# Fewer, larger transfers at both ends of a decode kernel, and a table load ahead of small transfers

## The chip, the cores and the metric

One core of a Trainium2 chip. The metric is device microseconds of one execution. The result is compared with executions of the kernel before made on the same chip in the same call (one batch of kernels, timed together). "Span" is the profiled time on the core, some 2 us shorter than the device time.

## The reference

A decode step for a batch of 8 (width 448): attention over the last 1024 positions of a key and value cache, a small MLP on the normalised input, and a gate that mixes the two.

```python
q = x @ wq                                   # 16 heads of 256
k, v = k_cache[:, :, -1024:], v_cache[:, :, -1024:]   # 8 kv heads, bf16
o = softmax(q k^T / 16) v                    # two query heads share one kv head
a = o.reshape(8, 4096) @ wo                  # wo: 4096 x 448
b = gelu(layernorm(x) @ w1 + b1) @ w2 + b2
out = g * a + (1 - g) * b,   g = sigmoid(sum(x * gate_w))
```

Keys and values are 67 MB, the weights wq, w1, w2 and wo 10.6 MB. All of it is read once.

## The kernel before

Every large load goes through a ring of nine slots of 128 x 8192 bf16, issued by the sync engine as slots come free. Keys and values come as 32 slots ("units") of 2 MB. The parts that the change touches:

```python
    WO_PARTS = [[(0, 4), (4, 8)]] * 2 + [            # row blocks of each quarter of wo,
        [(0, 4), (4, 6), (6, 8)],                    # 11 transfers in all
        [(0, 4), (4, 6), (6, 7), (7, 8)],
    ]
    ...
    add(("wq", 0), rows_loader([wq_m[:, 0 : 2 * HD]]))
    add(("wq", 1), rows_loader([wq_m[:, 2 * HD : 3 * HD], wq_t]))
    add_kv("k", A_k_cache, 0, parts=2)               # first keys in two halves
    ...                                              # w1, w2, then keys and values in turn
    for u in range(NQ - LAG, NQ):
        add_kv("v", A_v_cache, u, parts=2 if u == NQ - 1 else 1)   # last values in two halves
    ...
    pump()                                           # sync engine: issue what has a slot
    nc.scalar.dma_start(x_sb[:], xf)                 # ScalarE: four small transfers
    ...                                              # gate weights, b2, b1
    # GpSimd meanwhile: masks, and a long memset of qw
    # norm_and_gate():
        nc.vector.memset(eps_t[:], 1e-5)
        nc.scalar.activation(rstd[:], mv[:, 1:2], ACT.Sqrt, bias=eps_t[:], scale=1.0)
    ...
    # the end of the program
    values(u)                                        # last values
    gather(u)
    project(0, 0, 4)                                 # each piece of wo as it lands
    keep_clock(A_hi[:, W // 2 : W], 1)               # filler matmuls into an unused bank
    project(0, 4, NJ8)
    ...
    project(3)
    nc.vector.tensor_copy(res[:, 0:DH2], halves[0])
    nc.scalar.copy(res[:, DH2:D], halves[1])
    nc.sync.dma_start(out_f, res[:])
```

One thing that the source does not show: the built program gives each transfer, from either engine, one of eight completion semaphores in turn. A transfer waits until the earlier one with its semaphore has landed, so at most eight are under way: in the kernel before, for instance, the transfer issued at 176.51 us has the semaphore on which the last values landed at 176.49.

Of the kernel before, what the change touches and what calls it, by code (L numbers as in the profile page):

```python
# [8 lines left out]
ACT = mybir.ActivationFunctionType  # L9
# [3 lines left out]
F32 = mybir.dt.float32  # L13
# [5 lines left out]
def kernel(  # L19
# [15 lines left out]
    nc = tc.nc  # L35
    P = nc.NUM_PARTITIONS

    NB, Sq, D = A_x.shape
# [4 lines left out]
    W = min(4096, max(256, Sk // 4))  # L43
# [16 lines left out]
    NQ = NB * Hkv // QUAD  # L60
# [6 lines left out]
    HPQ = 4  # L67
    NHQ = Hq // HPQ
    NJ8 = HPQ * NJ
    WO_PARTS = [[(0, 4), (4, 8)]] * 2 + [  # L70
        [(0, 4), (4, 6), (6, 8)],
        [(0, 4), (4, 6), (6, 7), (7, 8)],
    ]
    RING = 9
    LAG = 2
    NK = 4
# [10 lines left out]
    consts = ctx.enter_context(tc.tile_pool(name="consts", bufs=1))  # L87
# [13 lines left out]
    def pump():  # L101
        while len(slots) < min(len(plan), consumed[0] + RING):
            t = ring.tile([P, SLOT], BF16, tag="slot", name="slot")
            plan[len(slots)](t)
            slots.append(t)
# [5 lines left out]
    def kv_loader(src, u, parts):  # L111
        b, half = divmod(u, Hkv // QUAD)
        v = src[b, half * QUAD : (half + 1) * QUAD, kv_base:Sk, :].rearrange(
            "a (s c) d -> s a (c d)", c=NCK
        )

        def load(t):
            n = NCK * Dh // parts
            for i in range(parts):
                nc.sync.dma_start(  # L120
                    t[:, i * n : (i + 1) * n], v[:, :, i * n : (i + 1) * n]
                )

        return load

    def rows_loader(pieces):
        def load(t):
            o = 0
            for ap in pieces:
                n = 1  # L130
                for s in ap.shape[1:]:
                    n *= s
                dst = t[:, o : o + n]
                if len(ap.shape) == 3:
                    dst = dst.rearrange("p (a n) -> p a n", a=ap.shape[1])
                nc.sync.dma_start(dst, ap)
                o += n

        return load
# [3 lines left out]
    def add(key, loader):  # L143
        index[key] = len(plan)
        plan.append(loader)

    def add_kv(name, src, u, parts=1):
        add((name, u), kv_loader(src, u, parts))
# [7 lines left out]

    add(("wq", 0), rows_loader([wq_m[:, 0 : 2 * HD]]))
    add(("wq", 1), rows_loader([wq_m[:, 2 * HD : 3 * HD], wq_t]))
    add_kv("k", A_k_cache, 0, parts=2)
    add(("w1",), rows_loader([w1_m, w1_t]))  # L160
    add(("w2",), rows_loader([w2_v]))
    for u in range(1, NQ):
# [1 line left out]
        if u >= LAG:  # L164
            add_kv("v", A_v_cache, u - LAG)
    for u in range(NQ - LAG, NQ):
        add_kv("v", A_v_cache, u, parts=2 if u == NQ - 1 else 1)
    for q in range(0, NHQ, 2):
        add(
            ("wo", q),  # L170
# [3 lines left out]
                    for i in range(2)  # L174
                    for j0, j1 in WO_PARTS[q + i]
                ]
# [3 lines left out]
    def slot(*key):  # L180
        return slots[index[key]]

    consts.tile([P, 112], BF16, name="pad")
    x_sb = consts.tile([NB, D], BF16)
    pump()
    nc.scalar.dma_start(x_sb[:], xf)
    gw_b = consts.tile([NB, D], BF16)
# [45 lines left out]
    def transposed(dst, src, srcz):  # L233
        tp = ps_misc.tile([P, NX, NB], BF16, tag="misc", name="tp")
        for r in range(NR):
            nc.tensor.transpose(tp[:, r, :], src[:, r:DM:NR], ident[:NB, :NB])
        for h in range(2):
            nc.tensor.transpose(tp[:, NR + h, :], srcz[:, h, :], ident[:NB, :NB])
        nc.vector.tensor_copy(dst[:], tp[:])
# [51 lines left out]
    def norm_and_gate():  # L291
        stats = consts.tile([NB, nc.vector.BN_STATS_DIM], F32)
        nc.vector.bn_stats(stats[:], x_sb[:])  # L293
        mv = consts.tile([NB, nc.vector.BN_AGGR_DIM], F32)
        nc.vector.bn_aggr(mv[:], stats[:])
        eps_t = consts.tile([NB, 1], F32)
        nc.vector.memset(eps_t[:], 1e-5)
        rstd = consts.tile([NB, 1], F32)
        nc.scalar.activation(rstd[:], mv[:, 1:2], ACT.Sqrt, bias=eps_t[:], scale=1.0)
        nc.vector.reciprocal(rstd[:], rstd[:])  # L300
        y_sb = consts.tile([NB, D], BF16)
        nc.vector.tensor_scalar(
            y_sb[:],
            x_sb[:],
            scalar1=mv[:, 0:1],
            scalar2=rstd[:],
            op0=ALU.subtract,
            op1=ALU.mult,
        )
        for h in range(2):  # L310
            nc.vector.tensor_copy(yz[:, h, h::2], y_sb[:, DM:D])
        transposed(yT, y_sb, yz)
        prod = consts.tile([NB, D], F32)
        gl = consts.tile([NB, 1], F32)
        nc.vector.scalar_tensor_tensor(
            prod[:],
            in0=x_sb[:],
            scalar=1.0,
            in1=gw_b[:],
            op0=ALU.mult,  # L320
            op1=ALU.mult,
            accum_out=gl[:],
        )
        gth = consts.tile([NB, 1], F32)
        nc.scalar.activation(gth[:], gl[:], ACT.Tanh, scale=0.5)
        nc.vector.tensor_scalar(
            gg[:, 0:1], gth[:], 0.5, 0.5, op0=ALU.mult, op1=ALU.add
        )
        nc.vector.tensor_scalar(
            gg[:, 1:2], gth[:], -0.5, 0.5, op0=ALU.mult, op1=ALU.add  # L330
        )
        nc.gpsimd.memset(each[:], 1.0)
        nc.vector.tensor_scalar_mul(each[:, 0:NB], ident[0:NB, 0:NB], gg[:, 0:1])
        gp = ps_misc.tile([P, NB], F32, tag="misc", name="gp")
        nc.tensor.matmul(  # L335
            gp[:], lhsT=each[:, NB : NB + P], rhs=each[:, 0:NB], start=True, stop=True
        )
        nc.vector.tensor_copy(gg_s[:], gp[:])
# [163 lines left out]
    def gather(u):  # L502
        first = soft.pop(u)
        os_ = epool.tile([P, Dh], F32, tag="os", name="os_")
        nc.vector.scalar_tensor_tensor(
            os_[:],
            in0=PO[:, 1, :],
            scalar=own[:, 1:2],
            in1=first[:],
            op0=ALU.mult,  # L510
            op1=ALU.add,
        )
        soft[u] = os_

    def finish(u):
        b, half = divmod(u, Hkv // QUAD)
        os_, rs = soft.pop(u), rsel.pop(u)
        sm = ps_sm.tile([P, NJ, RQ], F32, tag="sm", name="fin")
        for j in range(NJ):
            nc.tensor.matmul(  # L520
                sm[:, j, :], lhsT=os_[:, j::NJ], rhs=rs[:], start=True, stop=True
            )
        nc.scalar.activation(  # L523
            oT[:, half * RQ : (half + 1) * RQ, :, b].rearrange("p h j -> p j h"),
            sm[:],
            ACT.Copy,
            scale=gg_s[:, b : b + 1],
        )
# [64 lines left out]
    def keep_clock(dst, n):  # L593
        for _ in range(n):
            nc.tensor.matmul(dst, lhsT=foreign[:], rhs=place[:], start=True, stop=True)

    norm_and_gate()
    query()
    for hf in range(NH):
# [26 lines left out]
    u = NQ - 1  # L626
    A_lo = ps_misc.tile([NB, DH2], F32, tag="misc", name="A_lo")
    A_hi = ps_s.tile([P, W], F32, tag="S", name="A_hi")
# [15 lines left out]
    def spread_rows(q0, q1):  # L644
        pp = ps_sm.tile([P, HPQ, NJ, q1 - q0, NB], F32, tag="sm", name="pp")
        for i in range(HPQ):
            for m in range(HPQ):
                nc.tensor.matmul(
                    pp[32 * i : 32 * i + 32, m],
                    lhsT=ident[:, m::HPQ],  # L650
                    rhs=oTv[:, i, :, q0:q1, :],
                    start=True,
                    stop=True,
                )
        nc.vector.tensor_copy(
            oP[:, :, q0:q1, :], pp[:].rearrange("p m j q b -> p (m j) q b")
        )

    def project(q, j0=0, j1=NJ8):
        w = slot("wo", q - q % 2)  # L660
        for j in range(j0, j1):
            o = ((q % 2) * NJ8 + j) * D
            for i, dst in enumerate(halves):
                nc.tensor.matmul(  # L664
                    dst,
                    lhsT=oP[:, j, q, :],
                    rhs=w[:, o + i * DH2 : o + (i + 1) * DH2],
                    start=False,
                    stop=(q == NHQ - 1 and j == NJ8 - 1),
                    skip_group_check=True,  # L670
                )
# [19 lines left out]
    keep_clock(A_hi[:, W // 2 : W], 4)  # L691
    values(u)
    gather(u)
    project(0, 0, 4)
    keep_clock(A_hi[:, W // 2 : W], 1)
    project(0, 4, NJ8)
    finish(u)
    project(1, 0, 4)
    spread_rows(HALF, NHQ)
    project(1, 4, NJ8)  # L700
    keep_clock(A_hi[:, W // 2 : W], 1)
    project(2)
    keep_clock(A_hi[:, W // 2 : W], 1)
    project(3)

    nc.vector.tensor_copy(res[:, 0:DH2], halves[0])
# [32 lines left out]
```

## Time and profile before

| | |
|---|---|
| time, median of 3 | 190.5 us (190.38 to 190.54) |
| span of the profiled run | 188.4 us |
| bytes of the loads' queue | 77.67 MB |
| rate in the middle of the run | 429 to 432 GB/s |
| first large packet starts | 1.76 us |
| last completion of the output weights | 185.43 us |

The page of the kernel before lists issues by size, with the median time from issue to landing; these are the ones that the change merges:

```profile
q1 hardware_dynamic: 7360, 77.67, 97.3%
...
slot<-in_A_wo_dram SPq DMA_DIRECT2D x6, 448.0 KB, 26.5
...
slot<-in_A_k_cache_dram SPq DMA_DIRECT2D x2, 1024.0 KB
slot<-in_A_v_cache_dram SPq DMA_DIRECT2D x2, 1024.0 KB
```

The first line is the queue of the sync engine: packets, MB, and packet time as a share of 16 engines' span. Its 97.3% leave 5 us of the span, which are the start-up and the end. The 26.5 us from issue to landing is queueing: a piece of 0.45 MB takes about 1.1 us when its turn comes. The prediction shows the other lines.

### The profile page before, as it was taken

Reading aid. Unit: us, or ns where it says so; the run is one execution under the profiler, and the core shown is the slowest. Engines: PE = TensorE matmul, PEld = TensorE weight load, DVE = VectorE, ACT = ScalarE, POOL = GpSimd, SP = SyncE. Lnnn points to the kernel's source line nnn. Section 1 sums busy time; section 2 is a strip of 40 time slices with the busy share of each in tenths; the row PEclk is TensorE's granted clock in tenths of the full one; section 3 lists DMA queues with packets and bytes.
Section 4 is the critical chain, followed back from the end, with each engine's and each line's share of the span. In section 5 each row is a group of like instructions: output and inputs, shape, how many; then the busy total and the mean of one; then the engine's idle time right before and its main releaser. Section 6 shows DMA issues by size and latency. Waiting matters only on the chain.

```text
span 188.4 us, 2359 instructions
## 1 busy us (share of the span) xinstructions
PE 140.2 (74%) x945; PEld 70.3 (37%) x945; DVE 128.6 (68%) x178; ACT 45.1 (24%) x92; POOL 6.6 (4%) x14
## 2 busy tenths in 40 slices
PE   0027978998987589986758596849795999898983
PEld 0011863344434243433233243315242534345451
DVE  6960378979989494949494949595867768695300
ACT  2032220041340404040404040402240041325300
POOL 8500000000000000000000000000000000000000
PEclk9999999999999965799999699988999579999998
DMA  6999999999999999999999999999999999999991
GB/s 217 410 419 434 428 441 430 428 425 438 431 425 428 438 431 428 425 438 428 428 431 437 418 435 431 435 425 431 428 438 425 431 431 438 418 430 418 412 396 49
DMA packets 7548, 77.83 MB, mean 413 GB/s; under 512 B 985, under 2 KB 1778, under 8 KB 2674
## 3 DMA queue, kind: packets, MB, share of 16 engines
q1 hardware_dynamic: 7360, 77.67, 97.3%
q8 instruction: 7, 0.11, 0.2%
q10 hardware_dynamic: 178, 0.02, 0.1%
q14 instruction: 3, 0.02, 0.0%
HBM read 77.68 MB, written 0.01 MB: 412 GB/s over the span
## 4 chain that ended last, share of the span: by engine, by line
DMA 82%; DVE 9%; PE 4%; ACT 2%; issue 1%; DVEq 0%; SPq 0%; ACTq 0%
DMA slot<-in_A_k_cache_dram 59%; DMA slot<-in_A_v_cache_dram 18%; DMA slot<-in_A_wo_dram 4%; DVE kt L346 2%; DVE xz L242 2%; PE Sq L360 2%; ACT qw L401 1%; DMA x_sb<-in_A_x_dram 1%; DVE qw L403 1%; PE A_lo L664 1%; PE qt L375 1%; ACT qs L370 1%; PE qp L388 1%; PE gp L335 0%; DVE stats L293 0%
## 5 line engine op out<-in xcount | busy, mean ns | idle before, releaser
L346 DVE STREAM_TRANSPOSE kt<-slot 128x2048 int32<-128x2048 int32 x32 | 73.7, 2306 | 29.4 <-DMA slot<-in_A_k_cache_dram 29.4
L418 PE MATMUL S<-kt,qw 128*128 128x512 bf16 x256 | 69.4, 418 | 23.7 <-DVE kt L346 23.2
L418 PEld LDWEIGHTS <-qw 128*128 128x128 bf16 x256 | 26.4, 103 | 62.8 <-issue 41.9
L523 ACT ACTIVATE oT<-fin,gg_s 128x16 bf16<-128x16 f32 x16 | 5.2, 328 | 73.2 <-PE fin L520 73.2
L447 ACT ACTIVATE E<-S,nmx 128x1024 bf16<-128x1024 f32 x16 | 22.2, 1389 | 1.8 <-DVE nmx L444 1.7
L430 DVE TENSOR_REDUCE mx<-S 128x1 f32<-128x1024 f32 x16 | 19.0, 1188 | 0.1
L490 PE MATMUL PO<-slot,ET 128*16 128x512 bf16 x256 | 18.3, 410 | 0.3 <-DMA slot<-in_A_v_cache_dram 0.3
L499 ACT ACTIVATE first<-PO,own 128x256 f32<-128x256 f32 x16 | 7.6, 473 | 28.1 <-PE PO L490 28.1
L412 PE MATMUL S<-place,foreign 128*128 128x512 bf16 x32 | 13.4, 418 | 0.1
L460 DVE STREAM_TRANSPOSE ET<-E 128x512 int32<-128x512 int32 x16 | 11.2, 697 | 2.2 <-ACT E L447 2.2
L438 PE MATMUL mz<-m,same 128*128 128x4 f32 x32 | 6.4, 271 | 5.6 <-ACT oT L523 5.4
L438 PEld LDWEIGHTS mz<-m,same 128*128 128x128 f32 x32 | 5.2, 203 | 7.4 <-ACT oT L523 6.6
L471 PEld LDWEIGHTS den<-rowsum,rowden 128*128 128x128 f32 x32 | 6.7, 215 | 3.3 <-issue 1.0
L490 PEld LDWEIGHTS <-ET 128*16 128x16 bf16 x256 | 5.2, 91 | 5.3 <-issue 1.8
L412 PEld LDWEIGHTS <-foreign 128*128 128x128 bf16 x32 | 3.3, 102 | 9.2 <-issue 7.6
L664 PE MATMUL A_lo<-slot,oP 128*8 128x224 bf16 x32 | 4.8, 257 | 1.5 <-DMA slot<-in_A_wo_dram 1.2
L403 DVE CAST qw<-qp 32x512 bf16<-32x512 f32 x4 | 2.7, 687 | 3.4 <-ACT qw L401 3.4
L471 PE MATMUL den<-rowsum,rowden 128*128 128x1 f32 x32 | 5.0, 227 | 0.0
L482 ACT ACTIVATE rsel<-sel,rb 128x8 f32<-128x8 f32 x16 | 4.7, 292 | 1.0 <-DVE rb L481 1.0
L664 PE MATMUL A_hi<-slot,oP 128*8 128x224 bf16 x32 | 4.9, 259 | 0.0
L242 DVE COPY xz<-x_sb 8x64 bf16<-8x64 bf16 x2 | 4.1, 4030 | 0.5 <-DMA x_sb<-in_A_x_dram 0.5
L379 DVE COPY qd<-qt 128x64 bf16<-128x64 bf16 x4 | 0.6, 218 | 5.5 <-PE qt L375 5.5
(143 smaller groups left out, 105.3 us busy)
## 6 DMA issues: line engine op xcount, KB each, us to landing
slot<-in_A_k_cache_dram SPq DMA_DIRECT2D x15, 2048.0 KB, 36.9
slot<-in_A_v_cache_dram SPq DMA_DIRECT2D x15, 2048.0 KB, 36.8
slot<-in_A_wo_dram SPq DMA_DIRECT2D x6, 448.0 KB, 26.5
slot<-in_A_wq_dram SPq DMA_DIRECT2D x1, 2048.0 KB, 7.6
slot<-in_A_k_cache_dram SPq DMA_DIRECT2D x2, 1024.0 KB
slot<-in_A_v_cache_dram SPq DMA_DIRECT2D x2, 1024.0 KB
slot<-in_B_w_dram SPq DMA_DIRECT2D x1, 1568.0 KB
slot<-in_B_w_dram SPq DMA_DIRECT2D x1, 1344.0 KB, 11.8
```

The source lines that it names most:

```text
L242: nc.vector.tensor_copy(xz[:, h, h::2], x_sb[:, DM:D])
L346: nc.vector.transpose(kt[:].rearrange("p c k x r -> p (c k x r)").bitcast(WORD), kn[:, hf * CH * Dh : (hf + 1) * CH * Dh].bitcast(WORD),)
L412: nc.tensor.matmul(S[u][:, cols], lhsT=foreign[:], rhs=place[:], start=True, stop=False)
L418: nc.tensor.matmul(S[u][:, cols], lhsT=qw[:, j, u, m * RQ : m * RQ + P], rhs=kt[:, :, k, :, par], start=False, stop=(k == NK - 1 and par = ...
L430: nc.vector.reduce_max(mx[:], S[u][:], axis=AXIS.X)
L438: nc.tensor.matmul(mz[:], lhsT=same[:], rhs=m4[:], start=True, stop=True)
L447: nc.scalar.activation(E[:].rearrange("p c x i -> p c i x"), S.pop(u)[:].rearrange("p (c i x) -> p c i x", i=PAIR, x=BLK), ACT.Exp, bias=n ...
L460: nc.vector.transpose(ET[:].rearrange("p c r i -> p (c r i)").bitcast(WORD), E[:].rearrange("p c x i -> p (c x i)").bitcast(WORD),)
L471: nc.tensor.matmul(den[u][:], lhsT=rowden[:], rhs=rowsum[:], start=True, stop=True)
L490: nc.tensor.matmul(PO[32 * t : 32 * t + PAIR * RQ], lhsT=ET[:, c, 0:RQ, :], rhs=vn[:, PAIR * c * Dh : PAIR * (c + 1) * Dh], start=(c < QUA ...
L499: nc.scalar.activation(first[:], PO[:, 0, :], ACT.Copy, scale=own[:, 0:1])
L664: nc.tensor.matmul(dst, lhsT=oP[:, j, q, :], rhs=w[:, o + i * DH2 : o + (i + 1) * DH2], start=False, stop=(q == NHQ - 1 and j == NJ8 - 1), ...
```

## The change

The intent: larger transfers where the stream looked least efficient (the output weights), one transfer less at each end of the cache, and the table that Sqrt needs loaded before ScalarE begins its small transfers. With coarser weights, the end of the program is put in a simpler order.

```diff
-    WO_PARTS = [[(0, 4), (4, 8)]] * 2 + [
-        [(0, 4), (4, 6), (6, 8)],
-        [(0, 4), (4, 6), (6, 7), (7, 8)],
-    ]
+    WO_PARTS = [[(0, 8)]] * 3 + [[(0, 6), (6, 8)]]
@@
-    add_kv("k", A_k_cache, 0, parts=2)
+    add_kv("k", A_k_cache, 0)
@@
-        add_kv("v", A_v_cache, u, parts=2 if u == NQ - 1 else 1)
+        add_kv("v", A_v_cache, u)
@@
+    eps_t = consts.tile([NB, 1], F32)
+    rstd = consts.tile([NB, 1], F32)
+    nc.gpsimd.memset(eps_t[:], 1e-5)
+    nc.scalar.activation(rstd[:], eps_t[:], ACT.Sqrt)
     pump()
     nc.scalar.dma_start(x_sb[:], xf)
@@ (eps_t and its memset on VectorE, rstd: removed from norm_and_gate)
@@
-    project(0, 0, 4)
-    keep_clock(A_hi[:, W // 2 : W], 1)
-    project(0, 4, NJ8)
+    keep_clock(A_hi[:, W // 2 : W], 3)
     finish(u)
-    project(1, 0, 4)
+    project(0)
     spread_rows(HALF, NHQ)
-    project(1, 4, NJ8)
-    keep_clock(A_hi[:, W // 2 : W], 1)
+    project(1)
+    keep_clock(A_hi[:, W // 2 : W], 3)
     project(2)
-    keep_clock(A_hi[:, W // 2 : W], 1)
+    keep_clock(A_hi[:, W // 2 : W], 2)
     project(3)
```

More of the change, by code (lines that the diff above doesn't have):

```diff
@@ L295, in norm_and_gate @@
         nc.vector.bn_aggr(mv[:], stats[:])
-        eps_t = consts.tile([NB, 1], F32)
-        nc.vector.memset(eps_t[:], 1e-5)
-        rstd = consts.tile([NB, 1], F32)
         nc.scalar.activation(rstd[:], mv[:, 1:2], ACT.Sqrt, bias=eps_t[:], scale=1.0)
@@ L657, in spread_rows, with project @@
         )
-    def project(q, j0=0, j1=NJ8):
+    def project(q):
         w = slot("wo", q - q % 2)
-        for j in range(j0, j1):
+        for j in range(NJ8):
             o = ((q % 2) * NJ8 + j) * D
```

## The prediction

> **What bounds the kernel now.** I read the page from the top: busy shares first, then the slices, then the chain, and only then the timeline of the head and of the tail, because the change touches nothing in between.
>
> ```profile
> PE 140.2 (74%) x945; PEld 70.3 (37%) x945; DVE 128.6 (68%) x178; ACT 45.1 (24%) x92; POOL 6.6 (4%) x14
> ...
> DMA  6999999999999999999999999999999999999991
> GB/s 217 410 419 434 428 441 430 428 425 438 431 425 428 438 431 428 425 438 428 428 431 437 418 435 431 435 425 431 428 438 425 431 431 438 418 430 418 412 396 49
> ...
> DMA 82%; DVE 9%; PE 4%; ACT 2%; issue 1%; DVEq 0%; SPq 0%; ACTq 0%
> ```
>
> No compute engine is over 74%. The DMA row is 9 in every slice between the first and the last, and the chain that ended last is 82% transfers. So 77.67 MB (the bytes of queue q1 on the page) through the 16 DMA engines set the time, and compute only follows. The windows show how full the stream is, and where it is not at its best:
>
> ```profile
> 60.00:100.00 40.00, 30.59 (x186) 14.54 (x186) 29.17 (x33) 9.29 (x20) 0.00 (x0) 0.87 1.01 432
> ...
> 176.50:183.00 6.50, 5.62 (x83) 3.32 (x83) 0.78 (x2) 0.80 (x2) 0.00 (x0) 1.00 1.03 407
> ```
>
> The last two columns are DMA share and GB/s. In the stretch of keys and values the engines are full (1.01) at 432 GB/s; in the stretch of the output weights they are as full (1.03), yet move 407. Full but slower means a cost per packet, not a wait. After the stream comes only a short tail:
>
> ```profile
> 184.83 0.26 PE L664 MATMUL A_lo<-slot,oP 128*8 128x224 bf16 x1
> ...
> 185.19 0.26 PE L664 MATMUL A_lo<-slot,oP 128*8 128x224 bf16 x1
> ...
> 185.48 0.26 PE L664 MATMUL A_lo<-slot,oP 128*8 128x224 bf16 x1
> ...
> 185.77 0.38 DVE L706 CAST res<-A_lo 8x224 bf16<-8x224 f32 x1 [4.74 <-PE A_hi L664]
> 185.80 0.34 ACT L707 CAST res<-A_hi 8x224 bf16<-8x224 f32 x1 [5.54 <-PE A_hi L664]
> 186.22 0.35 SPq L708 DMA_DIRECT2D out_dram<-res  x1
> ```
>
> Each of those matmuls starts as its own small piece of weights lands (the trace counts the last completion of the last piece at 185.43 us). From there to the end of the span, 188.4 us, are 2.9 us that the change leaves alone but for the last matmuls. The head looks like this:
>
> ```profile
> 0.73 0.58 ACTq L186 DMA_DIRECT2D x_sb<-in_A_x_dram  x1
> 0.73 1.35 SPq L136 DMA_DIRECT2D slot<-in_A_wq_dram  x3
> ...
> 2.36 1.28 ACT L299 ACT_TABLE_LOAD   x1 [2.36 <-issue]
> 2.61 4.35 POOL L289 MEMSET qw<- 128x5120 bf16 x1
> ...
> 2.95 4.10 DVE L242 COPY xz<-x_sb 8x64 bf16<-8x64 bf16 x2 [0.48 <-DMA x_sb<-in_A_x_dram]
> ...
> 10.46 0.29 ACT L299 ACTIVATE rstd<-mv,eps_t 8x1 f32<-8x1 f32 x1 [6.81 <-DVE eps_t L297]
> ```
>
> The table load ends at 3.64 us, and its user runs at 10.46: the load is already hidden. The two tiny copies of x start at 2.95 us and end only at 7.06, 0.1 us after GpSimd's long memset of qw (2.61 + 4.35 = 6.96).
>
> **What the Trainium skill says.** (1) "DMA: Bandwidth & Descriptors", section "Bandwidth", asks for transfers of 1 MiB or more and puts a floor of about 10.5 ns on a packet; section "Why small descriptors are slow (HBM only)" names a fixed cost per packet. The trace agrees in kind and shows a smaller number: packets of 16384, 8192, 3584, 1792 and 896 bytes took 611, 309, 141, 75 and 42 ns (medians of the packet records), which is about 7 to 9 ns plus 36.9 ps per byte. (2) The same page, section "Queues, rings and completion order", says that an engine takes turns between the rows of its queues, a packet at a time. The trace agrees: the 28-byte packets of b1 sit between large ones, and the gate weights, issued at 1.35 us, have most of their packets only at 5.6 to 6.8 us, behind weights of wq that were queued before them. (3) "SBUF — State Buffer", section "Who interferes with whom": a VectorE copy in a two-port mode and a GpSimd operation exclude each other for a whole instruction. The 4.03 us for an 8x64 copy, ending with the memset, agree. (4) "ScalarE: Activation LUTs", section "What ACT_TABLE_LOAD costs", gives 1283 ns; both loads here took 1283 ns.
>
> **The change part by part.**
>
> *Transfers.* Output weights go from 11 to 5, first keys and last values from 2 to 1 each: 8 transfers fewer. Every transfer has a row per partition, 128 packets, so 8 per engine, plus one completion packet per engine of 9 ns. (Check: 51 loads x (128 + 16) and 16 completions of the store are 7360, the page's count for q1.)
> - Output weights, before, per engine: 8 x (6 x 140.7 + 3 x 74.6 + 2 x 41.6) ns = 9.21 us, with the mean times of the packet records.
> - After: rows of 7168 and 5376 bytes, which the line above puts at 271 and 205 ns: 8 x (3 x 271 + 205 + 75) ns = 8.75 us. Gain 0.46 us.
> - Keys and values in one: 2 x 8 x (2 x 309 - 611) ns = 0.11 us. Eight completion packets: 8 x 9 ns = 0.07 us.
> - Sum of packet times: 0.64 us.
>
> Packets overlap a little (shares of 1.01 to 1.03), so this is an upper figure. A lower one comes from landings: the output weights took 176.49 to 185.43 us = 8.94 us, and their 3.67 MB at 430 GB/s would take 8.53. That excess of 0.41 us belongs to 88 data and 11 completion packets less the 16 or so that keys and values have for as many bytes, so about 5 ns each; 72 packets per engine fewer (64 data, 8 completion) give 0.36 us. I take the middle, **0.5 us**, and all of it lies on the stream, which is the path.
>
> *The tail.* The last piece holds two row blocks instead of one: one more pair of matmuls, 0.09 us apart in the timeline, after the last landing. **+0.1 us.** The projection of the third part now waits for a whole 0.9 MB, but 16 matmuls take some 0.8 us and such a part lands every 2.1 us, so TensorE catches up each time. The first six blocks of the last part take 6 x 0.095 = 0.57 us, about what the last piece takes to land (0.60 us), so they just fit. Fillers in this stretch grow from 3 to 8 matmuls of 0.21 us, which fill waits and keep the clock.
>
> *The last values in one.* The first half of that matmul group could start a half transfer earlier before; but the trace shows all 16 starting at 176.55, after both halves. Cost 0.
>
> *The head.* ScalarE now does a table load (1.28 us) and one small activation (0.29 us) before it issues x: at about 0.73 + 1.6 = 2.35 us instead of 0.73. By then wq is queued, so x waits behind it as the gate weights did (over 4 us): I expect it to land at 6.5 to 7.5 us instead of 2.85. Most of this is free, because the copies of x are held until 7.06 us by the memset anyway; the first query matmul loses 0 to 0.8 us. This is hidden: the key transfer that follows the head in the chain is issued at 31.19 and lands at 64.35, so 33 us of transfers are queued ahead of it. The early table load saves nothing on the path. Moving x away from the front of the queues could start wq earlier by up to 0.1 us (its first packets start at 1.76 us, those of x at 1.68); I count 0.
>
> Total: -0.5 + 0.1 = **-0.4 us**, 190.5 to 190.1.
>
> **The rivals.** *A larger gain, by 1 us or more:* if each transfer cost a fixed setup on the stream, 8 fewer would give it. Against it: the engines are full to 1.03 in that very stretch, so completions of one transfer overlap the next one. It would give 189.5. *The late x becomes the bound:* x, then wq's release, then later issues. For it: x is on the chain at its start, and eight semaphores shared by all transfers make later issues wait for earlier landings, now also for the late small ones. Against it: four transfers (5.8 MB) are queued before the first such wait, good for over 13 us. It would give 190.5 to 191.5. *Coarse pieces stall the end:* TensorE idles, its clock halves, and the last six blocks plus two take twice as long: +0.8 us, so 190.8. Against it: the granted clock was 1.00 up to 186 us and the fillers increase.
>
> **Range and chances.** The packet estimate runs from 0.36 to 0.64 us, the tail may cost 0 to 0.4, and the three runs before spread by 0.16 us. Predicted 190.1 us, eight times in ten within 189.6 to 190.5. Two per cent are 3.8 us, more than the whole tail after the stream; nothing in the change reaches that either way: faster 0.01, same 0.98, slower 0.01.
>
> **What would show it.** Right: queue q1 with 1152 packets fewer (6208); the stretch of output weights above 415 GB/s; last landing near 185.0 instead of 185.43 us; x landing after 6 us with the first key transposes at most 1 us later, and the GB/s row unbroken. Wrong: a hole in the DMA row near 10 to 30 us (the late x reached the stream), a granted clock under 1 after 178 us, or a last landing that has not moved, which would say that the packet cost was not on the slowest engine's path.

## The result, and the profile after

190.14 us median (189.78 to 190.49, four runs) against 190.52 (190.38 to 190.61, four runs). The ratio is 0.9981, 95% interval 0.9961 to 1.0000: same at two per cent. Ratios here are the mean time of one kernel's runs over that of the other's runs of the same rounds, so they are not quite the ratio of the medians. Later: 190.29 against 190.44 and 190.21 against 190.42. Over the 14 executions, the differences of the means are 0.37, 0.17 and 0.22 us, on average **0.24 us** weighted by runs.

The page of the changed kernel, against the rows in the prediction: rates, the loads' queue and the chain.

```profile
GB/s 210 417 435 428 436 425 426 432 432 432 428 428 435 428 435 428 428 432 428 432 437 425 421 439 435 421 432 439 425 425 435 439 428 425 425 442 432 409 392 38
...
q1 hardware_dynamic: 6208, 77.67, 97.1%
...
DMA 76%; DVE 15%; PE 4%; ACT 2%; issue 1%; DVEq 0%; ACTq 0%; SPq 0%
```

Same bytes in 6208 packets instead of 7360, and no hole in the stream. The chain's share of transfers falls from 82% to 76% and that of VectorE rises from 9% to 15%. That is no shift of the bound: the chain goes back through whichever event released each slot, and the rates of the stream are unchanged. The windows of the changed kernel, with DMA share and GB/s last:

```profile
60.00:100.00 40.00, 29.39 (x187) 14.25 (x189) 29.09 (x33) 9.63 (x21) 0.00 (x0) 0.89 1.01 430
...
176.50:183.00 6.50, 4.89 (x73) 2.92 (x75) 0.78 (x2) 0.81 (x2) 0.00 (x0) 1.00 1.00 416
```

The middle is as before; the stretch of the output weights rises from 407 to 416 GB/s. The head, in order of time (start, duration, engine; ACTq and SPq are the sequencers that issue transfers):

```profile
0.73 1.28 ACT L185 ACT_TABLE_LOAD   x1 [0.73 <-PEq L719]
...
0.86 0.58 ACTq L187 DMA_DIRECT2D x_sb<-in_A_x_dram  x1
...
2.03 0.20 ACT L185 ACTIVATE rstd<-eps_t 8x1 f32<-8x1 f32 x1
...
2.65 4.36 POOL L290 MEMSET qw<- 128x5120 bf16 x1
...
4.58 2.51 DVE L243 COPY xz<-x_sb 8x64 bf16<-8x64 bf16 x2 [2.10 <-DMA x_sb<-in_A_x_dram]
...
7.38 0.18 DVE L240 COPY xT<-tp 128x40 bf16<-128x40 bf16 x1 [0.28 <-PE tp L239]
```

The issue of x starts at 0.86 us, *while* the table load runs (0.73 to 2.01), not after it. Even so x lands at 4.5 us instead of 2.85: it now stands behind the first packets of wq, which take 1.0 to 1.7 us each at the start (packet records), where before it was 0.08 us ahead of them. The copies of x still end at 7.09 us, when the memset ends at 7.01, so the transposed x is ready at 7.56 instead of 7.51.

The tail, the projection of the last quarter:

```profile
184.69 0.26 PE L662 MATMUL A_lo<-slot,oP 128*8 128x224 bf16 x1
...
185.26 0.26 PE L662 MATMUL A_lo<-slot,oP 128*8 128x224 bf16 x1
...
185.35 0.26 PE L662 MATMUL A_lo<-slot,oP 128*8 128x224 bf16 x1
...
185.65 0.38 DVE L702 CAST res<-A_lo 8x224 bf16<-8x224 f32 x1 [4.96 <-PE A_hi L662]
```

The six-block piece has landed by 184.65 and the last piece at 185.18 (completion records). The first six blocks just fit between; the last two follow at 185.26 and 185.35. The copy of the result starts at 185.65 instead of 185.77 us: 0.12 us gained, which is 0.25 at the last landing less 0.13 for the extra block behind it.

### The profile page after: what moved, and what is told of

The parts are those of the page before. It is cut to its first block, busy times and chain, and to the rows that moved or that the text cites. A ratio compares the mean times of both kernels' runs of the same rounds, so it can differ in the third digit from the quotient of the medians.

```text
span 188.2 us, 2351 instructions
## 1 busy us (share of the span) xinstructions
PE 132.2 (70%) x938; PEld 68.0 (36%) x950; DVE 126.7 (67%) x177; ACT 45.4 (24%) x93; POOL 6.7 (4%) x15
## 3 DMA queue, kind: packets, MB, share of 16 engines
q1 hardware_dynamic: 6208, 77.67, 97.1%
## 4 chain that ended last, share of the span: by engine, by line
DMA 76%; DVE 15%; PE 4%; ACT 2%; issue 1%; DVEq 0%; ACTq 0%; SPq 0%
DMA slot<-in_A_k_cache_dram 40%; DMA slot<-in_A_v_cache_dram 20%; DMA slot<-in_A_wo_dram 15%; DVE kt L344 7%; DMA x_sb<-in_A_x_dram 2%; PE Sq L358 2%; DVE xz L243 1%; ACT qw L399 1%; DVE mx L428 1%; DVE qw L401 1%; ACT qs L368 1%; PE A_lo L662 0%; PE qp L386 0%; PE qt L373 0%; DVE ET L458 0%
## 5 line engine op out<-in xcount | busy, mean ns | idle before, releaser
L416 PE MATMUL S<-kt,qw 128*128 128x512 bf16 x256 | 66.0, 402 | 31.0 <-DVE kt L344 28.5
L416 PEld LDWEIGHTS <-qw 128*128 128x128 bf16 x256 | 25.6, 100 | 66.3 <-issue 43.9
L488 PE MATMUL PO<-slot,ET 128*16 128x512 bf16 x256 | 17.5, 395 | 0.3 <-DMA slot<-in_A_v_cache_dram 0.3
L410 PE MATMUL S<-place,foreign 128*128 128x512 bf16 x25 | 9.8, 390 | 0.1
L410 PEld LDWEIGHTS <-foreign 128*128 128x128 bf16 x32 | 3.2, 99 | 8.6 <-issue 6.9
L662 PE MATMUL A_lo<-slot,oP 128*8 128x224 bf16 x32 | 3.7, 258 | 1.2 <-DMA slot<-in_A_wo_dram 1.1
L290 POOL MEMSET qw<- 128x5120 bf16 x1 | 4.4, 4355 | 0.0
L593 PEld LDWEIGHTS <-foreign 128*128 128x128 bf16 x33 | 2.9, 99 | 3.6 <-issue 0.8
L593 PE MATMUL idle<-place,foreign 128*128 128x512 bf16 x16 | 4.1, 378 | 0.1
```

Source lines behind the costliest of these rows:

```text
L410: nc.tensor.matmul(S[u][:, cols], lhsT=foreign[:], rhs=place[:], start=True, stop=False)
L416: nc.tensor.matmul(S[u][:, cols], lhsT=qw[:, j, u, m * RQ : m * RQ + P], rhs=kt[:, :, k, :, par], start=False, stop=(k == NK - 1 and par = ...
L488: nc.tensor.matmul(PO[32 * t : 32 * t + PAIR * RQ], lhsT=ET[:, c, 0:RQ, :], rhs=vn[:, PAIR * c * Dh : PAIR * (c + 1) * Dh], start=(c < QUA ...
L593: nc.tensor.matmul(dst, lhsT=foreign[:], rhs=place[:], start=True, stop=True)
```

## The experiments

**Theory A:** the stream of transfers is full, each packet costs it about 5 ns, and the change takes away 72 packets per engine (64 data, 8 completion); nothing else in it matters but one more pair of matmuls at the end. **Rivals:** F, a fixed cost per transfer; H, the head carries the gain or loses some; N, scatter; and, for the end, that fillers keep the clock up. V came up on the way: something in the combination makes the weights alone slower.

A single execution scatters by 0.2 us or more, about as much as the effect. So beside the time I read one number from the completion records of each trace: when the 16 DMA engines each finish the last piece of output weights, as mean, and as the slowest of the 16, which is the one that the matmuls wait for.

| run | large transfers | mean engine, us | slowest engine, us | median, us (before) |
|---|---|---|---|---|
| before | 51 | 184.52 | 185.43 | 190.52 |
| changed | 43 | 184.12 | 185.18 | 190.14 (190.52) |
| after_again | 43 | 184.22 | 185.38 | 190.29 (190.44) |
| after_third | 43 | 184.27 | 185.23 | 190.21 (190.42) |
| wo_only | 45 | 184.24 | 185.04 | 190.81 (190.44) |
| wo_only_2 | 45 | 184.17 | 185.21 | 190.42 (190.42) |
| wo_old | 49 | 184.48 | 185.32 | 190.54 (190.44) |
| preload_only | 51 | 184.54 | 185.54 | 190.37 (190.44) |
| no_preload | 43 | 184.10 | 185.13 | 190.25 (190.42) |
| x_late | 43 | 184.14 | 185.18 | 190.14 (190.42) |
| no_fill | 43 | 184.19 | 185.09 | 190.25 (190.42) |
| kv_halves | 75 | 185.62 | 186.58 | 191.54 (190.42) |
| wo_runs | 43 | 185.22 | 186.39 | 191.24 (190.42) |
| wo_fine | 70 | 190.57 | 191.21 | 196.50 (190.42) |

### The parts of the change, one at a time

**after_again**, the changed kernel unedited:

> The changed kernel once more, as the yardstick of this call. Theory A (fewer packets on a full stream): 0.3 to 0.5 us faster than before, ratio 0.9975 to 0.9985. Rival N (the first measurement was scatter, 189.78 to 190.49 over four runs): ratio 0.999 to 1.001.

Ratio 0.9991 (0.9978 to 1.0003): by time alone, this does not separate theory A from N. The mean engine is 0.30 us earlier than before, though.

**wo_only**: the output weights and the end of the program as changed, the rest as before (edit against the changed kernel, shortened, as in the other runs).

```diff
-    add_kv("k", A_k_cache, 0)
+    add_kv("k", A_k_cache, 0, parts=2)
-        add_kv("v", A_v_cache, u)
+        add_kv("v", A_v_cache, u, parts=2 if u == NQ - 1 else 1)
-    nc.scalar.activation(rstd[:], eps_t[:], ACT.Sqrt)     # and the rest of the early table load
```

> Only the output weights in 5 transfers and the end of the program that goes with it; first keys, last values and the table load as before. Theory A: removes 48 of the 64 data packets and 6 of the 8 completions per engine, so packet times of the loads' queue fall by 0.5 us of the whole change's 0.58 us, and most of the gain is here: 0.25 to 0.4 us faster than before. Rival H (the head gives the gain): ratio 1.000.

The stream did as theory A said: 184.24 us on the mean engine, 0.28 earlier. The time did not: ratio 1.0018 (1.0004 to 1.0032), slightly slower though the same at two per cent.

**wo_old**: the complement, output weights and end of the program as before, the rest changed.

```diff
-    WO_PARTS = [[(0, 8)]] * 3 + [[(0, 6), (6, 8)]]
+    WO_PARTS = [[(0, 4), (4, 8)]] * 2 + [[(0, 4), (4, 6), (6, 8)], [(0, 4), (4, 6), (6, 7), (7, 8)]]
     # and the end of the program of the kernel before
```

> The changed kernel with the output weights in 11 transfers and the end of the program as before. Theory A: 16 data packets and 2 completions per engine fewer than before, 0.1 us of packet time; 0 to 0.15 us faster than before. Rival H (first keys in one transfer and the early table load carry the gain): 0.3 to 0.4 us faster than before.

Ratio 1.0001 (0.9988 to 1.0013), mean engine 0.04 us earlier. The time also carries 0.13 us of closing waits that the kernel before does not have (last column of the table further down: 0.21 against 0.08 us). Without them this run would be about 0.1 us faster, as theory A expects for its 18 packets per engine, and short of the 0.3 us of rival H. So the first keys, the last values and the table load carry at most a small part of the gain; rival H falls.

**preload_only**: the kernel before with the early table load and nothing else.

```diff
+    nc.gpsimd.memset(eps_t[:], 1e-5)                      # edit against the kernel before
+    nc.scalar.activation(rstd[:], eps_t[:], ACT.Sqrt)
     pump()
     nc.scalar.dma_start(x_sb[:], xf)
     # ... eps_t and its memset on VectorE, rstd: removed from norm_and_gate
```

> Only the early table load on top of the kernel before. Theory A: x lands near 4.5 us instead of 2.85 because its packets fall behind the first weights, the transposed x is ready within 0.1 us of before because the copies of x wait for GpSimd's memset anyway, and the time is the same: ratio 0.9995 to 1.0005. Rival H: 0.2 us or more either way.

Ratio 0.9995 (0.9982 to 1.0007). Its head, in order of time, shows the late x and what hides it:

```profile
0.86 0.59 ACTq L190 DMA_DIRECT2D x_sb<-in_A_x_dram  x1
...
2.65 4.36 POOL L293 MEMSET qw<- 128x5120 bf16 x1
...
4.52 2.58 DVE L246 COPY xz<-x_sb 8x64 bf16<-8x64 bf16 x2 [2.04 <-DMA x_sb<-in_A_x_dram]
...
7.37 0.18 DVE L243 COPY xT<-tp 128x40 bf16<-128x40 bf16 x1 [0.28 <-PE tp L242]
```

### What one packet costs, and one transfer

These runs enlarge the suspected cost, so that the time can show it. Their increases are given over x_late, which is the changed kernel but for the place of x (190.14 us).

**kv_halves**: every transfer of keys and values in two.

```diff
-    def add_kv(name, src, u, parts=1):
+    def add_kv(name, src, u, parts=2):
```

> The changed kernel with every transfer of keys and values cut in two: 32 transfers more, of 8 data packets and one completion per engine each. Theory A (a cost per packet): packet times rise by 32 x (8 x 7 + 9) ns = 2.1 us per engine, and the time by 1.4 (5 ns a packet, from landings) to 2.1 us over the changed kernel, to 191.5 to 192.2 us. Rival F (a fixed cost per transfer on the stream, 0.38 us for 8 transfers): 32 x 0.048 = 1.5 us, not told apart here, but it is by the next run. Rival N (packets overlap, nothing on the path): under 0.3 us.

191.54 us, ratio to before 1.0069 (1.0053 to 1.0085): 1.40 us more, at the low end of what theory A allows. On the mean engine the stream ends at 185.62 us, 1.45 later than the average, 184.17, of the six profiles that have exactly the change's large transfers (changed, after_again, after_third, no_preload, no_fill, x_late). For 32 x 9 = 288 packets per engine, that is 5.0 ns each. The window over the middle of this kernel, against 429 to 430 GB/s of the changed one:

```profile
100.00:140.00 40.00, 28.94 (x169) 13.45 (x173) 27.84 (x32) 10.00 (x23) 0.00 (x0) 0.92 1.01 426
```

**wo_runs**: the five transfers of the output weights, but with a gap after each row block in the slot, so that a partition's part is no longer one run.

```diff
-                dst = t[:, o : o + n]                                  # 3584 columns in a row
+                dst = t[:, o * 512 : (o + n) * 512].rearrange("p (a n) -> p a n", n=512)[:, :, 0:D]
     # ... the source cut into row blocks to match
-            o = ((q % 2) * NJ8 + j) * D
+            o = ((q % 2) * NJ8 + j) * 512
```

> The changed kernel's five transfers of output weights, each partition's part now in runs of 896 bytes with gaps between them in the slot: 256 data packets per engine instead of 40, no transfer more. Theory A: packet times rise by 256 x 41.6 ns - 8.75 us = 1.9 us; the time rises by 1.1 (5 ns each) to 1.9 us. Rival F (cost per transfer): no change against the changed kernel.

191.24 us, 1.10 more, with not one transfer added: rival F falls. On the mean engine 185.22 - 184.17 = 1.05 us for 216 packets, 4.9 ns each. The queue of the loads on its page:

```profile
q1 hardware_dynamic: 9664, 77.67, 97.4%
```

and the window over the output weights:

```profile
176.50:183.00 6.50, 5.00 (x74) 2.89 (x74) 0.78 (x2) 0.80 (x2) 0.00 (x0) 1.00 1.09 377
```

More packets for the same bytes, and engines that are full (1.09) and slower: 377 GB/s instead of 416. That is the signature that the prediction had read in the kernel before, enlarged.

**wo_fine**: one transfer per row block.

```diff
-    WO_PARTS = [[(0, 8)]] * 3 + [[(0, 6), (6, 8)]]
+    WO_PARTS = [[(j, j + 1) for j in range(8)]] * 4
```

> Output weights in 32 transfers of one row block: the same 256 data packets per engine as the run with gaps, and 27 transfers more. Theory A: as the run with gaps plus 27 x 9 ns = 0.25 us. Rival F: 27 x 0.048 = 1.3 us more than the run with gaps. A third possibility: only eight transfers, 0.9 MB or 2.1 us of stream, may be under way at a time, so the stream runs dry and the time rises by several us with a low DMA share at the end.

196.50 us, 5.3 over wo_runs with the same data packets. The third possibility came true in its outcome, as the windows over the end show (DMA share and GB/s last, granted clock before them):

```profile
176.50:183.00 6.50, 4.80 (x68) 2.45 (x67) 0.78 (x2) 0.80 (x2) 0.00 (x0) 1.00 0.77 217
183.00:191.00 8.00, 5.99 (x38) 1.73 (x37) 0.00 (x0) 0.00 (x0) 0.00 (x0) 0.63 0.80 219
```

The DMA share is 0.77 and 0.80, not 1.0, at half the rate: the stream lacks work. What paces it is the issuing, though, and not the number under way. The same trace, asked for the transfers of output weights by line and by time:

```profile
L133 SPq DMA_DIRECT2D slot<-in_A_wo_dram x32: 327/430/957, 142.4 to 188.5; - x32
```

```profile
176.38 12.55 SPq L133 DMA_DIRECT2D slot<-in_A_wo_dram  x25
```

The first line has the least, median and greatest ns of one issue, the second the start and length of the last 25 together. The eight semaphores hold 24 of the 32 back until the last values have landed, and then the sync engine issues them one by one, about every 0.474 us from 180 us on. None of those issues waits for its semaphore, whose earlier transfer had landed at least 0.9 us before. By these numbers 0.115 MB every 0.474 us are 242 GB/s, an estimate somewhat above the 217 and 219 of the windows. A packet cost (wo_runs) looks full and slow; a lack of queued work looks partly empty. The granted clock falls to 0.63 in the second stretch, where TensorE waits.

### The head with a late x

**x_late**: x issued behind all of the query weights, by the sync engine.

```diff
-    nc.scalar.dma_start(x_sb[:], xf)
+    def wq1_then_x(t):
+        wq1(t)
+        nc.sync.dma_start(x_sb[:], xf)
     # ... and further down
-    nc.scalar.dma_start(x_sb[:], xf)
```

> The changed kernel with x issued by the sync engine behind all of the query weights. x lands near 10.5 us instead of 4.5, so the transposed x and the queries come some 3 us later. Theory A (33 us of transfers are queued behind the head): time within 0.3 us of the changed kernel, no hole in the DMA row. Rival H (the head is on the path): 2 to 3 us slower.

190.14 us, ratio 0.9989 (0.9974 to 1.0004), like the changed kernel. x was even later than expected, in order of time:

```profile
12.12 0.24 PE L242 MATMUL tp<-ident,x_sb 8*128 8x8 bf16 x3 [12.12 <-DMA x_sb<-in_A_x_dram]
...
12.75 0.18 DVE L245 COPY xT<-tp 128x40 bf16<-128x40 bf16 x1 [0.28 <-PE tp L244]
```

and the window after the head:

```profile
31.00:60.00 29.00, 25.18 (x135) 11.15 (x137) 28.00 (x32) 6.80 (x13) 0.00 (x0) 0.91 1.00 429
```

The transposed x came 5.4 us later, and the stream ran on at 429 GB/s. The head is hidden, with room to spare.

### Why the weights alone did not gain, and the fillers

**after_third**, the changed kernel again, as the yardstick:

> The changed kernel, as the yardstick of this call. Theory A: the mean over the 16 engines of the last completion of the output weights is 0.3 to 0.4 us below the kernel before (184.52 us), as in its three profiles so far (184.12, 184.22, and 184.14 with x late); the time 0.15 to 0.4 us faster than before.

Ratio 0.9987 (0.9974 to 0.9999), mean engine 184.27, just inside the expected gain.

**wo_only_2**, the run with the weights alone again:

> Repeats the run with the output weights alone, which came out 0.26 us slower in four unprofiled executions although its profile showed the stream ending 0.28 us earlier on the mean engine. Theory A with scatter from elsewhere: 0.1 to 0.35 us faster than before this time, mean engine near 184.25. Rival V (halved first keys and last values, or the late table load, really cost with coarse weights): again 0.2 to 0.3 us slower than before.

190.42 us, ratio 1.0001 (0.9987 to 1.0014): neither expectation. The stream again ended early (184.17 us), and the time again did not follow. The difference lies after the last matmul. Both profiles of this kernel need 3.11 to 3.12 us from the start of their last pair of matmuls to the end of the span; the profiles of before and of the changed kernel need 2.88 to 2.90. The sync engine closes the program with five waits, each for two semaphores, in an order that the build fixes. From the trace's records of them, in us:

```
kernel      output landed   the wait it ends     waits left   closing drain starts   landed to drain
before          187.52      fifth of five            0              187.60               0.08
changed         187.40      fifth of five            0              187.49               0.08
no_preload      187.34      fifth of five            0              187.42               0.08
wo_old          187.38      third of five            2              187.59               0.21
wo_only         187.25      second of five           3              187.53               0.28
wo_only_2       187.46      second of five           3              187.74               0.28
```

Each wait left over takes 0.06 to 0.07 us even though its transfer landed long ago. Which wait the output ends depends on which of the eight semaphores falls to it, and so on the number of transfers in the program. In the runs with the weights alone it costs 0.2 us: together with the 0.1 us of the longer last piece, that is the 0.3 us that the stream had gained. Theory A's stream holds; its step from stream to time lacked this term. The extra 0.26 us of slowness in the first wo_only's times, which the second did not repeat, stays open; its own profiled execution took 190.37 us.

**no_preload**, the changed kernel with the table load where it was:

```diff
-    nc.gpsimd.memset(eps_t[:], 1e-5)
-    nc.scalar.activation(rstd[:], eps_t[:], ACT.Sqrt)
+        nc.vector.memset(eps_t[:], 1e-5)        # in norm_and_gate, as before
```

> The changed kernel without the early table load. Theory A: the same as the changed kernel within 0.15 us, x lands near 2.9 us again. Rival V, if the table load is what matters: slower than before by 0.2 to 0.3 us, like the run with the output weights alone.

Ratio 0.9984 (0.9971 to 0.9996), no slower than the changed kernel. x lands by 2.35 us. The table load is not what helps, and the half of rival V that blames its late place falls. The other half, the halved first keys and last values, was not tested alone; in both runs with the weights alone the stream ended as early as theory A says, and the closing waits explain the second one.

**no_fill**, the changed kernel without the eight fillers:

```diff
-    keep_clock(A_hi[:, W // 2 : W], 3)    # and the two other calls after the last values
```

> The changed kernel without the 8 filler matmuls after the last values. If they keep the clock: granted clock under 1 after 180 us, the last 16 projection matmuls 0.2 us apart instead of 0.09, and 0.3 to 0.8 us slower. Rival: gaps of under 2 us don't lower the clock, and the time is that of the changed kernel within 0.15 us.

Ratio 0.9990 (0.9977 to 1.0002), the time of the changed kernel. The window over the whole end:

```profile
179.00:186.00 7.00, 4.12 (x83) 3.28 (x82) 0.67 (x2) 0.67 (x2) 0.00 (x0) 1.00 0.69 282
```

The granted clock (before the last two columns) stayed 1.00, although TensorE was busy for 4.12 of 7 us instead of 5.25 in the changed kernel. These fillers are not needed.

### What stays between the mean engine and the time

Until 23.8 us the 16 engines of the changed kernel complete each transfer within 0.55 to 0.57 us of each other. At 24.4 us a packet of 16384 bytes appears on another queue, which the page lists as instructions; in the next transfer the last engine is 1.90 us behind the first instead of 0.55, and it stays so. Seven such packets come by the end, and one engine after another falls back; at the end seven of the 16 are more than 1.5 us behind the first. Before and wo_fine show the same step at the same place (0.56 to 1.69, 0.66 to 1.42). The lag shrinks only slowly (before: 1.69 us at 28.8 us, 1.55 at 67.7), and the last matmuls wait for the slowest. That is why the slowest engine scatters (185.09 to 185.38 with the change's five weight transfers and the rest as in the changed kernel) more than the mean (184.10 to 184.27). x_late moves the first of these packets, to 29.95 us, and the step moves with it: the transfer landing from 28.6 us still spreads over 0.55 us, and of the next, from 33.5 us, 15 engines finish within 0.56 us and the last 2.0 us behind the first. In the other thirteen traces the packet comes at 24.4 to 25.5 us and the step in the transfer then under way. No run removed the packets, so how much of the time they cost stays open.

No experiment pointed to a version that beats both kernels by more than the scatter. Taking the fillers out gives the same time with less work.

## Why the prediction was right or wrong

- **What bounds it**: right. x_late, kv_halves and wo_runs all say so: the head may slip by 5 us for nothing, and anything that lengthens the stream shows in full.
- **Transfers, 0.5 us**: the mechanism was right, packets on a full stream, and the size was somewhat too large. The mean engine ends 0.36 us earlier (184.53 for the two profiles with all of before's transfers, 184.17 for the six with the change's), which is the lower of the two figures worked out, 72 packets of 5 ns. The term that was mis-sized is the upper one: packet durations overstate the path because packets overlap. The sum of durations fell by 0.58 us (183.30 to 182.72 us per engine, packet records), close to the 0.64 worked out, but that is not time on the path. Taking the middle of the two was the mistake; of two figures, the one from landings counts.
- **Last landing at 185.0**: 185.18. On the slowest engine the gain averages 0.28 us (185.48 to 185.20), with scatter that the mean engine does not have.
- **The tail, +0.1**: right, 0.13 us.
- **The last values in one, 0**: consistent. All 16 of their matmuls start together at 176.45 us, as before at 176.55.
- **The head**: the outcome was right, one step was wrong. The prediction had ScalarE issue x at 2.35 us, behind table load and activation; it was issued at 0.86 us, because the sequencer goes on to the next instruction while its engine works. x landed at 4.5 us, not after 6, and for another reason than the late issue: 0.13 us were enough to put it behind the first packets of wq.
- **Fillers keep the clock**: they are not needed here. Without them (no_fill) the granted clock was 1.00 too, so the rival of coarse pieces stalling the end at a lower clock falls.
- **Rivals**: a gain of 1 us or more from fixed costs per transfer is excluded by kv_halves, where 32 transfers more cost 1.40 us, which is 0.35 for 8, packets included; the late x as the bound, by x_late.
- **The total, 0.4 us**: 0.38 between the medians of the first call, 0.24 on average over three calls. That the first call agrees so well is luck: 0.28 on the slowest engine less 0.13 at the tail gives 0.15, and the rest of the 0.24 is within the scatter of single executions.
- **What was not in the sum**: the order of the closing waits. The changed kernel was lucky in it, as before was: nothing was added. With two transfers more (wo_only) it would have cost 0.2 us, half of the predicted gain.
- **Slips in the readings**, none of which moves the total: 141, 75 and 42 ns are rounded means (140.7, 74.6, 41.6), the medians are 140, 74 and 41. The store's 16 packets are 8 of data and 8 completions. And only the packets of b1 bear out the turns between queues. The gate weights' own eight packets came at 5.5 to 5.8 us (the one at 6.8 is b2's), 4 us after their issue, which a turn of one packet of wq (0.6 to 1.7 us) does not explain; why stays open.

## What to carry to other kernels

On a stream that is full from end to end, count packets: here a longer run per partition paid about 5 ns per packet and engine saved, and the number of transfers paid nothing beyond its own completion packets, as long as the issuing kept ahead of the stream. Judge gains of a few tenths of a microsecond by the completions of all the DMA engines, and read the path after the last landing too, down to the closing waits. A rearranged head was worth nothing here, with 33 us of transfers queued ahead of what it releases.

## What the Trainium skill lacked or had wrong

- "DMA: Bandwidth & Descriptors", section "Bandwidth", gives about 10.5 ns per packet (for the other way of issuing, from GpSimd). Here a packet more on a full stream cost 5.0 ns (kv_halves) and 4.9 ns (wo_runs) of time.
- "Runtime: NRT & Kernel Launch", section "Instruction fetch mechanics", says that instructions are fetched in blocks of 16 KiB and that crossing a block's end is mostly hidden. The trace agrees with the block (16384 bytes, seven times). It adds a cost that the page lacks: the spread of the 16 engines' completions goes from 0.55 to 1.90 us after the first such packet and is still 1.78 us for the transfer at 67.5 us; in x_late packet and step came 5 us later together.
- "ScalarE: Activation LUTs", section "What ACT_TABLE_LOAD costs", adds a drain of about 1380 ns to the 1283 ns of the load. Here the activation after the early load starts at 2.03 us, 0.02 us after the load's end (0.73 + 1.28), so no drain showed there. It is the first load of the program, not a switch in mid-work.
- "Perfetto Trace Analysis", section "DVE / Act Engine Instruction (TENSOR_ADD, Activation, etc)", has the sequencer free to decode the next instruction once one is pushed. The trace agrees, and it matters for transfers: one behind a table load on ScalarE was issued 0.13 us after the load began.
- No page has the order of the program's closing waits: 0.06 to 0.07 us for each wait that stands behind the output's.
